# Other first fillers on TensorE, another order of VectorE's work, and a filler moved, in a state-space block followed by an MLP

## The chip, the cores and the metric

The kernel runs on one core of a Trainium2 chip. Its time is the device time of one execution in microseconds; of several executions the median counts. A profiled execution also gives a trace: what each engine did, when, and what it waited for. The engines are TensorE (PE, with its weight loads as PEld), VectorE (DVE), ScalarE (ACT), GpSimd (POOL) and SyncE (SP, which only issues DMAs here). They run side by side, each through its own queue in order, and wait for each other by semaphores.

## The reference

Two blocks one behind the other, all in float32 (`S` = 768, `D` = 32, `N` = 16, 4 batches of 8 heads):

```python
log_a = np.log(np.clip(a, 1e-06, 1.0))
for c in range(nc):                          # chunks of 32 steps
    cum = np.cumsum(la, axis=-1)
    L = np.exp(cum[:, :, :, None] - cum[:, :, None, :]) * causal
    M = np.einsum('bhin,bhjn->bhij', Cc, Bc) * L
    y_intra = np.einsum('bhij,bhjd->bhid', M, xc)
    y_inter = np.einsum('bhin,bhnd->bhid', Cc, state) * np.exp(cum)[..., None]
    y[:, :, sl] = y_intra + y_inter
    state = decayed state + sum over the chunk of B x, decayed to its end
h = x @ w_in                                 # x: y as (3072, 256); w_in (256, 2048)
g = h * (1.0 / (1.0 + np.exp(-1.702 * h)))
return (g @ w_out).astype(np.float32)        # w_out (2048, 256)
```

The weights reach the kernel as 64-bit floating-point numbers, as pairs of 32-bit words.

## The kernel before

The 3072 tokens are worked in 6 groups of 512 (128 steps of all four batches). The kernel uses chunks of 64 steps instead of 32, which gives the same result. For a group, the first block gives `yT`, the transposed input of the second; the second makes 16 blocks of 128 hidden columns from it (`hidden`, L791 for the first group) and projects them to the output. From the second group on, the matrix products are split by a scheme of seven products instead of eight, with sums of operands made by VectorE (`first`, `product`, L847 to L956). The first group has plain products, because the weights are still being prepared.

No scheduler decides the order: the kernel is written in the order in which each engine is to run, and `in_order` ties each engine's instructions to that order. The order below is therefore the order in each queue.

**The start, on TensorE.** `dense` (L424) multiplies a matrix of ones by itself, in float32, into a bank that nothing reads afterwards or, with `start=False`, into unused columns of a bank in use; `pads` (L417) does so with 4 columns and a 32x32 tile. At L1056 to L1067 the queue is: two `dense` of 192 columns, the eight mask products (`mask`, L500, 16-bit operands), three `dense`, 27 `pads`. Then `differ_of(0)` and `differ_of(1)` (L506), which read the running sums `cum` that VectorE scans (L362), `rows_first` (L495), `score` (L604, result `cb`) and `turn_back` (L562). Float32 products show two records each in the trace.

**The exponents.** ScalarE takes `decay_exp` (L536) of the differences, once for the first pair of batches and four times for the second; VectorE multiplies the result with `cb` (`weigh`, L615), which gives `L`.

**The rows.** `finish(range(PG), (0,))` and `(1,)` make the first group's `yT`. Step 0 is a `dense` of 256 columns and `intra` of the first pair (L729; its two halves t = 0, 1 of the heads go to different banks). Step 1 is, for each t, `intra` of the second pair, a copy by ScalarE (`copied`, L741), `inter` (L716, needs the state that `gain`, L635, and `keep_first`, L651, make) and another copy. At t = 0 a second `dense` of 256 columns stands behind `intra`. The banks of t = 1 were those of `turn_back`, which VectorE reads in `ends_first` (L467, result `Be`); so `intra` of t = 1 waits for `Be`.

**The weights.** `fetch` loads the weights in ten pieces; the first six hold `w_in`, of 2, 2, 2, 2, 4 and 4 blocks. Piece 0 comes in two halves of one block each. The 64-bit numbers are taken apart and rounded to float32 with integer and float operations: `fields` step 0 cuts out the exponent field (L203, into `p`), step 1 the top of the mantissa (L206, into `m`), `rounded` adds the low word (L222), `clamp` (L215, L217) moves the exponent to the float32 range on ScalarE, and `join` puts in the sign (L236) and multiplies (L242, into `w_in`). A memset of one element on VectorE ahead of a load (`held`, L170) sets when SP may issue it. The exponents of piece 0 are handled in two halves: field and clamp of half 0 ahead of `ends_first`, field and clamp of half 1 behind it (L1098 to L1103).

Of the kernel before, what the change touches and what calls it, by code (L numbers as in the profile page):

```python
# [8 lines left out]
FP32 = mybir.dt.float32  # L9
# [7 lines left out]
P = 128  # L17
# [18 lines left out]
def kernel(  # L36
# [154 lines left out]
    def columns(i, half):  # L191
        n = PIECES[i][2] * DM
        return slice(0, n) if half is None else slice(half * n // 2, (half + 1) * n // 2)

    def fields(i, steps=range(2), half=None):
        cols = slice(0, PIECES[i][2] * DM)
        if i not in power:
            mantissa[i] = wide.tile([P, PN], U32, tag="m", name=f"m{i}")[:, cols]
            power[i] = wide.tile([P, PN], U32, tag="p2", name=f"p2{i}")[:, cols]
        cols = columns(i, half)  # L200
        hi = bits[i][1][:, cols]
        if 0 in steps:
            nc.vector.tensor_scalar(out=power[i][:, cols], in0=hi, scalar1=0x7FF00000, scalar2=None,  # L203
                                    op0=ALU.bitwise_and)
        if 1 in steps:
            nc.vector.tensor_scalar(out=mantissa[i][:, cols], in0=hi, scalar1=0x000FFFFF,  # L206
                                    scalar2=0x00100000, op0=ALU.bitwise_and, op1=ALU.bitwise_or)

    def clamp(i, steps=range(2), half=None):


        e = power[i][:, columns(i, half)]
        z = e.bitcast(FP32)
        if 0 in steps:
            nc.scalar.activation(z, e, AF.Relu, scale=-8.0, bias=edge[:, 0:1])  # L215
        if 1 in steps:
            nc.scalar.activation(e, z, AF.Relu, scale=-1.0, bias=edge[:, 1:2])  # L217

    def rounded(i, half=None):

        cols = columns(i, half)
        nc.vector.scalar_tensor_tensor(out=mantissa[i][:, cols].bitcast(FP32), in0=bits[i][0][:, cols],  # L222
                                       scalar=2.0 ** -32, in1=mantissa[i][:, cols],
                                       op0=ALU.mult, op1=ALU.add)
# [192 lines left out]
    def pads(n, t, start=True):  # L417

        for i in range(n):
            c = 32 * (i % R)  # L420
            nc.tensor.matmul(out=t[c:c + 32, :4], lhsT=ones[:32, :32], rhs=ones[:32, :4],
                             start=start, stop=True, tile_position=(0, c), skip_group_check=True)

    def dense(t, n=4, start=True):  # L424
        nc.tensor.matmul(out=t[:, :n * H], lhsT=ones,
                         rhs=ones[:, :H].unsqueeze(1).to_broadcast([P, n, H]),
                         start=start, stop=True, skip_group_check=True)

    def decay_heads(p, r, ab):

# [33 lines left out]
    def ends_first(p):  # L464

        t = ssd.tile([P, R, 2 * Q, N], FP32, tag="Be", name=f"Be{p}", bufs=3)
        nc.vector.tensor_tensor(  # L467
            out=t, in0=rb[p], in1=drops[:, p].unsqueeze(3).to_broadcast([P, R, 2 * Q, N]), op=ALU.mult)
        BE[p] = t.rearrange("p r (k q) n -> p k r (q n)", k=2), t
# [140 lines left out]
    def weigh(p, ks=(slice(0, 2),)):  # L610

        Lv = Ls[p].rearrange("p k r q i -> p k r (q i)")
        cb = st[p]["cb"].rearrange("p r k e -> p k r e")
        for k in ks:
            nc.vector.tensor_tensor(out=Lv[:, k], in0=Lv[:, k], in1=cb[:, k], op=ALU.mult)  # L615
# [66 lines left out]
    def finish(pairs, steps=range(2)):  # L682


        g, first = divmod(pairs[0], PG)
        early = pairs[0] < PG
        if 0 in steps:
            if early:
                banks = begun_y["banks"] = [bank(f"y0_{i}") for i in range(4)]
                y = [t[:, :2 * P].rearrange("p (k i) -> p k i", i=H) for t in banks]  # L690
                begun_y[0] = [[y[2 * t + i] for t in range(NK)] for i in range(2)], set()
            else:
                both = area(f"y{pairs[0]}")[:, :, :len(pairs) * 2 * H].rearrange(
                    "p (s t) (k i) -> p s t k i", s=2, i=H)
                begun_y[pairs[0]] = [[both[:, i, t] for t in range(NK)] for i in range(2)] + [both], set()
        y, begun = begun_y[pairs[0]]

        def begin(i, t, parts):
            new = not begun & {(i, t, q) for q in parts}
            begun.update((i, t, q) for q in parts)  # L700
            return new

        def inter(n, p, ts=range(2)):

            b = place(p)[1]
            for k in range(2):
                for i in range(2):
                    if g == 0 and i == 0:
                        continue
                    old = (state[g][:, 0] if i else state[g - 1][:, 1])[:, b + k]  # L710
                    for r in range(R):
                        t = r // 2
                        if t not in ts:
                            continue
                        rows, to = slice(32 * r, 32 * r + 32), Q * D * (r % 2)
                        nc.tensor.matmul(  # L716
                            out=y[i][t][to:to + Q * D, 2 * n + k], lhsT=old[rows],
                            rhs=st[p]["CsT"][rows, k, SIDES[i]],
                            start=begin(i, t, range(Q * (r % 2), Q * (r % 2) + Q)), stop=early,
                            tile_position=(32 * r, to), skip_group_check=True)  # L720

        def intra(n, p, ts=range(2)):
            L = Ls[p]
            for k, t in [(k, t) for t in ts for k in range(2)] if early else [
                    (k, t) for k in range(2) for t in ts]:
                for q in range(HB):
                    h = t * HB + q
                    for i, side in enumerate(SIDES):
                        nc.tensor.matmul(  # L729
                            out=y[i][t][D * q:D * q + D, 2 * n + k], lhsT=rx[p][side, k, h],  # L730
                            rhs=L[side, k, h // Q, h % Q],
                            start=begin(i, t, (q,)), stop=not early, tile_position=(H * i, D * q),
                            skip_group_check=True)

        cols = slice(2 * first * P, 2 * (first + len(pairs)) * P)

        if first == 0 and g not in yT:
            yT[g] = ffn.tile([P, NK, TG], FP32, tag="yT", name=f"yT{g}")
        if early:
            def copied(i, t):  # L740
                nc.scalar.activation(  # L741
                    yT[g][:, t, cols].rearrange("p (k s i) -> p s k i", s=2, i=H)[:, i], y[i][t],
                    AF.Copy)

            if 0 in steps:
                dense(begun_y["banks"][0][:, 2 * P:])
                intra(0, pairs[0])
                return
            for t in range(NK):
                intra(1, pairs[1], (t,))  # L750
                if t == 0:
                    dense(begun_y["banks"][0][:, 2 * P:])
                copied(0, t)
                for n, p in enumerate(pairs):
                    inter(n, p, (t,))
                copied(1, t)
        else:
            for step in steps:
                for n, p in enumerate(pairs):
                    (inter, intra)[step](n, p)  # L760
            if 1 not in steps:
                return
            for i in range(2):
                nc.scalar.activation(  # L764
                    yT[g][:, :, cols].rearrange("p t (k s i) -> p s t k i", s=2, i=H)[:, i], y[2][:, i],
                    AF.Copy)
        state.pop(g - 1, None)
        for p in pairs:
            st.pop(p)
            Ls.pop(p)  # L770
# [283 lines left out]
        differ(p, [(r, ab[p, r]) for r in range(R)])  # L1054

    busy = bank("busy")  # L1056
    for k in range(2):
        dense(busy, 3)
    both = area("ab0")
    for r in range(R):  # L1060
        mask_banks(0, r, both[:, r])
    seconds = [bank(f"ab1_{r}") for r in range(R)]
    for r in range(R):
        mask_banks(1, r, seconds[r])
    for r in range(3):
        dense(both[:, r, 2 * P:], 3, False)
    pads(27, both[:, 0, 2 * P:], False)  # L1067
    differ_of(0)
    turn_blocks(0, "C")
    fetch(0, held=nc.vector, halves=(0,))  # L1070
# [24 lines left out]
    weigh(0, (slice(0, 1),))  # L1095
    fetch(1, held=nc.vector)
    weigh(0, (slice(1, 2),))
    fields(0, (0,), 0)  # L1098
    clamp(0, half=0)
    for p in range(PG):  # L1100
        ends_first(p)
    fields(0, (0,), 1)
    clamp(0, half=1)  # L1103
    for i in range(2, 6):
        fetch(i, held=nc.vector if i == 2 else None)
    rows = a.rearrange("b h s -> (b h) s")
# [10 lines left out]
    keep_first(0)  # L1117
    finish(range(PG), (1,))
    join(0, 2, (0,))
    fields(0, (1,), 1)  # L1120
    rounded(0, 1)
    join(0, 2, (1,))
    fields(1)
    clamp(1)
# [240 lines left out]
```

## Time and profile before

| what | value |
|---|---|
| median of 3 runs | 352.63 us (351.96 to 353.89) |
| the profiled execution | 349.35 us |
| its span, first to last instruction | 347.6 us |
| TensorE busy | 341.9 us, 98% |
| VectorE busy | 256.2 us, 74% |
| ScalarE busy | 150.2 us, 43% |
| GpSimd busy | 46.0 us, 13% |
| granted TensorE clock | 0.999 |
| TensorE's first product, first product of `hidden` | 1.21 us, 17.27 us |

In a line of the timeline the first number is the start in us from the beginning of the span, the second the length, then engine, line, operation, output and inputs, shape and how many records were merged; in brackets, how long the engine had been idle before, and what released it. TensorE's products overlap, so a merged line is somewhat longer than its records are apart. A line of the chain of waits has start, length, and the work or wait that decided there. The page's slices (8.7 us each) show VectorE busy at nine tenths or more from 17.4 to 87 us, and the DMA engines from 17.4 to 52 us.

### The profile page before, as it was taken

To read this page: it belongs to the slowest core of one execution; us is meant where nothing else is said; L and a number is where in the kernel's file an instruction comes from. 1 tells how busy PE (TensorE), PEld (TensorE's weight loads), DVE (VectorE), ACT (ScalarE), POOL (GpSimd) and SP (SyncE) were. 2 spreads that over 40 slices of the span, in tenths; PEclk is the share of its full clock that TensorE was granted. 3 is DMA by queue.
4 is the path that set the end of the run, shared out by engine and by line. 5 is a ranking of instruction groups with operands and counts; after the bars stand their busy time and mean duration, and the time that the engine had idled before them with its cause. 6 is when DMAs were issued, how large, how long until landed. Compare 5 with 4: busy or idle time off the path is not lost.

```text
span 347.6 us, 8544 instructions
## 1 busy us (share of the span) xinstructions
PE 341.9 (98%) x3514; PEld 281.7 (81%) x3514; DVE 256.2 (74%) x479; ACT 150.2 (43%) x335; POOL 46.0 (13%) x82
## 2 busy tenths in 40 slices
PE   8899999999999999999999999999999999999996
PEld 7668964555788888888888888888888888899996
DVE  7799999999699897839985648985554653555463
ACT  6689664005354314644332543442444322554320
POOL 8306810300495000000000000000000000000000
PEclk9999999999999999999999999999999999999999
DMA  4799995713638000474123345120000120000221
GB/s 106 220 297 287 286 158 126 117 25 76 101 87 139 2 0 17 78 136 80 29 35 64 44 102 98 24 32 7 2 4 0 19 35 9 0 2 0 33 31 60
DMA packets 82831, 25.79 MB, mean 74 GB/s; under 512 B 68856, under 2 KB 81144, under 8 KB 82792
## 3 DMA queue, kind: packets, MB, share of 16 engines
q1 hardware_dynamic: 79912, 23.19, 31.5%
q0 software_dynamic: 1888, 1.74, 2.8%
q8 instruction: 27, 0.44, 0.5%
q10 hardware_dynamic: 992, 0.33, 0.4%
q14 instruction: 12, 0.10, 0.1%
HBM read 21.99 MB, written 3.24 MB: 73 GB/s over the span
## 4 chain that ended last, share of the span: by engine, by line
PE 90%; DVE 5%; DMA 2%; issue 1%; SPq 0%; DVEq 0%
PE acc L949 28%; PE X L847 19%; PE Y L857 14%; PE o L889 8%; PE acc L956 7%; PE h L791 6%; PE y L729 2%; PE cb L604 2%; PE y L716 2%; DMA bits<-in_moe_w_in_dram 1%; PE A L635 1%; DVE p L236 1%; DVE p L203 1%; DVE w_in L242 1%; DMA zC<-in_C_dram 1%
## 5 line engine op out<-in xcount | busy, mean ns | idle before, releaser
L852 ACT ACTIVATE ac<-X 128x256 f32<-128x256 f32 x76 | 29.1, 383 | 79.8 <-PE X L847 79.4
L949 PE MATMUL acc<-mg,mw 128*128 128x256 f32 x192 | 54.5, 379 | 0.0
L976 DVE TENSOR_TENSOR gT<-Y,ac 128x512 f32<-128x512 f32 x38 | 26.2, 690 | 37.1 <-PE Y L857 33.3
L824 ACT ACTIVATE gT<-gT 128x512 f32<-128x512 f32 (+1 forms) x76 | 39.3, 519 | 31.6 <-DVE gT L976 31.0
L847 PE MATMUL X<-my,mi 128*128 128x256 f32 x152 | 45.1, 379 | 0.0
L976 DVE TENSOR_TENSOR gT<-Y,b 128x256 f32<-128x256 f32 x38 | 15.8, 418 | 34.4 <-PE Y L857 34.4
L949 PEld LDWEIGHTS acc<-mg,mw 128*128 128x128 f32 x192 | 36.5, 190 | 5.0
L791 PE MATMUL h<-yT,w_in 128*128 128x128 f32 (+2 forms) x186 | 36.3, 353 | 0.2 <-DVE w_in L242 0.2
L949 PE MATMUL acc<-gT,w_out 128*128 128x256 f32 x128 | 35.5, 379 | 0.0
L791 PEld LDWEIGHTS h<-yT,w_in 128*128 128x128 f32 x186 | 27.1, 191 | 8.4 <-issue 5.5
L847 PEld LDWEIGHTS X<-my,mi 128*128 128x128 f32 x152 | 28.0, 190 | 3.7
L889 PE MATMUL o<-gT,w_out 128*128 128x512 f32 x64 | 28.6, 597 | 0.0
L815 DVE TENSOR_TENSOR mg<-gT 128x512 f32<-128x512 f32 x40 | 27.2, 680 | 0.0
L949 PEld LDWEIGHTS acc<-gT,w_out 128*128 128x128 f32 x128 | 24.2, 190 | 3.4 <-ACT yT L764 0.2
L852 ACT ACTIVATE b<-X 128x256 f32<-128x256 f32 x38 | 14.6, 384 | 20.6 <-PE X L847 20.2
L847 PE MATMUL X<-yT,w_in 128*128 128x256 f32 x76 | 23.2, 389 | 0.0
L857 PE MATMUL Y<-yT,w_in 128*128 128x256 f32 x76 | 22.7, 381 | 0.0
L857 PE MATMUL Y<-my,mi 128*128 128x256 f32 x76 | 22.6, 379 | 0.0
L847 PE MATMUL X<-my,w_in 128*128 128x256 f32 x76 | 22.6, 381 | 0.0
L857 PE MATMUL Y<-yT,mi 128*128 128x256 f32 x76 | 22.5, 379 | 0.0
L889 PEld LDWEIGHTS o<-gT,w_out 128*128 128x128 f32 x64 | 11.8, 190 | 13.2 <-issue 12.7
L1008 POOL DMA_DIRECT2D out_dram<-ob x32 | 17.4, 551 | 26.8 <-DVE ob L1003 26.1
(142 smaller groups left out, 580.2 us busy)
## 6 DMA issues: line engine op xcount, KB each, us to landing
a<-scratch SPq DMA_DIRECT2D x18, 256.0 KB
bits<-in_moe_w_out_dram SPq DMA_DIRECT2D x8, 512.0 KB
x<-in_x_dram SPq DMA_DIRECT2D x20, 128.0 KB
bits<-in_moe_w_in_dram SPq DMA_DIRECT2D x8, 256.0 KB
bits<-in_moe_w_in_dram SPq DMA_DIRECT2D x4, 512.0 KB
out_dram<-ob SPq DMA_DIRECT2D x128, 16.0 KB
af<-in_a_dram SPq DMA_DIRECT2D x20, 64.0 KB
zC<-in_C_dram SPq DMA_DIRECT2D x36, 32.0 KB
```

The lines of the kernel that those rows point to most:

```text
L604: nc.tensor.matmul(out=s["cb"][side, r, k].rearrange("p (q i) -> p q i", q=Q), lhsT=BT[rows, k, side], rhs=CT[rows, k, :, side], start=Tru ...
L791: nc.tensor.matmul(out=h[:, cols], lhsT=w_in[:, f, k], rhs=yT[g][:, k, cols], start=(k == 0 and e == 0), stop=(k == NK - 1), skip_group_ch ...
L815: nc.vector.tensor_tensor(out=t[:, 0:2], in0=B[:, :, 1], in1=B[:, 0], op=ALU.subtract)
L824: nc.scalar.activation(o, i, AF.Silu, scale=GELU_SCALE)
L847: nc.tensor.matmul(out=s["X"], lhsT=lhsT, rhs=rhs, start=i == "1", stop=i == "4", skip_group_check=True)
L852: nc.scalar.activation(copy, s["X"], AF.Copy)
L857: nc.tensor.matmul(out=o, lhsT=lhsT, rhs=rhs, start=s.pop("new", False), stop=i != "5", skip_group_check=True)
L889: nc.tensor.matmul(out=o[c], lhsT=w_out[:, c, f], rhs=gT[g, f // 2][:, f % 2], start=(f == 0), stop=(f == NF - 1), skip_group_check=True)
L949: nc.tensor.matmul(out=acc[g][0][i], lhsT=w, rhs=h, start=(j == 0 and (i, 0) in begins), stop=(j == NF // 2 - 1), skip_group_check=True)
L956: nc.tensor.matmul(out=o[k] if type(o) is list else o[:, cols], lhsT=h[:, cols], rhs=w, start=(j == 0 and (i, k) in begins), stop=(j == NF ...
L976: nc.vector.tensor_tensor(out=o, in0=v, in1=w, op=ALU.add)
L1008: (nc.sync if g else nc.gpsimd).dma_start(out=rows[:, b, :, cols], in_=t[32 * r:32 * r + 32, b * P:(b + 1) * P].rearrange("p (u e) -> p u ...
```

## The change

Four edits at the start of the kernel:

1. The first fillers. Both groups of `dense` in front of and behind the masks (2 and 3 float32 products of 192 columns) give way to `plain`: 6 products of 256 columns each, of a 16-bit constant 1.0 that the framework writes (POOL memset, from 0.38 us). One pad fewer (26).
2. `ends_first` of both pairs now stands ahead of the exponent field and clamp of piece 0's half 0.
3. The field of half 1 is cut out together with its mantissa, behind `join` of half 0, and its clamp is made by two VectorE operations (`clamp_here`) behind its rounding, instead of two ScalarE activations.
4. The second 256-column `dense` goes from step 1 of `finish` (behind `intra` of the second pair, t = 0) to step 0: a `dense` now stands before each half t of `intra` of the first pair.

The instructions of the other engines, and the DMAs, keep their order. The parameter `engine` of `fields` is used with its default only.

```diff
--- before.py
+++ after.py
@@ -192,7 +192,7 @@
         n = PIECES[i][2] * DM
         return slice(0, n) if half is None else slice(half * n // 2, (half + 1) * n // 2)
 
-    def fields(i, steps=range(2), half=None):
+    def fields(i, steps=range(2), half=None, engine=nc.vector):
         cols = slice(0, PIECES[i][2] * DM)
         if i not in power:
             mantissa[i] = wide.tile([P, PN], U32, tag="m", name=f"m{i}")[:, cols]
@@ -200,11 +200,20 @@
         cols = columns(i, half)
         hi = bits[i][1][:, cols]
         if 0 in steps:
-            nc.vector.tensor_scalar(out=power[i][:, cols], in0=hi, scalar1=0x7FF00000, scalar2=None,
+            engine.tensor_scalar(out=power[i][:, cols], in0=hi, scalar1=0x7FF00000, scalar2=None,
                                     op0=ALU.bitwise_and)
         if 1 in steps:
             nc.vector.tensor_scalar(out=mantissa[i][:, cols], in0=hi, scalar1=0x000FFFFF,
                                     scalar2=0x00100000, op0=ALU.bitwise_and, op1=ALU.bitwise_or)
+
+    def clamp_here(i, half):
+
+        e = power[i][:, columns(i, half)]
+        z = e.bitcast(FP32)
+        nc.vector.tensor_scalar(out=z, in0=e, scalar1=8.0, scalar2=float(896 << 23),
+                                op0=ALU.mult, op1=ALU.subtract)
+        nc.vector.tensor_scalar(out=e, in0=z, scalar1=0.0, scalar2=float(255 << 23),
+                                op0=ALU.max, op1=ALU.min)
 
     def clamp(i, steps=range(2), half=None):
 
@@ -425,6 +434,13 @@
         nc.tensor.matmul(out=t[:, :n * H], lhsT=ones,
                          rhs=ones[:, :H].unsqueeze(1).to_broadcast([P, n, H]),
                          start=start, stop=True, skip_group_check=True)
+
+    def plain(t, n, start=True):
+
+        for i in range(n):
+            nc.tensor.matmul(out=t[:, :2 * P], lhsT=nc.const_aps.tensor(1.0, [P, P], BF16),
+                             rhs=nc.const_aps.tensor(1.0, [P, 2 * P], BF16),
+                             start=start, stop=True, skip_group_check=True)
 
     def decay_heads(p, r, ab):
 
@@ -743,13 +759,12 @@
                     AF.Copy)
 
             if 0 in steps:
-                dense(begun_y["banks"][0][:, 2 * P:])
-                intra(0, pairs[0])
+                for t in range(NK):
+                    dense(begun_y["banks"][0][:, 2 * P:])
+                    intra(0, pairs[0], (t,))
                 return
             for t in range(NK):
                 intra(1, pairs[1], (t,))
-                if t == 0:
-                    dense(begun_y["banks"][0][:, 2 * P:])
                 copied(0, t)
                 for n, p in enumerate(pairs):
                     inter(n, p, (t,))
@@ -1054,17 +1069,15 @@
         differ(p, [(r, ab[p, r]) for r in range(R)])
 
     busy = bank("busy")
-    for k in range(2):
-        dense(busy, 3)
+    plain(busy, 6)
     both = area("ab0")
     for r in range(R):
         mask_banks(0, r, both[:, r])
     seconds = [bank(f"ab1_{r}") for r in range(R)]
     for r in range(R):
         mask_banks(1, r, seconds[r])
-    for r in range(3):
-        dense(both[:, r, 2 * P:], 3, False)
-    pads(27, both[:, 0, 2 * P:], False)
+    plain(both[:, 0, 2 * P:], 6, False)
+    pads(26, both[:, 0, 2 * P:], False)
     differ_of(0)
     turn_blocks(0, "C")
     fetch(0, held=nc.vector, halves=(0,))
@@ -1095,12 +1108,10 @@
     weigh(0, (slice(0, 1),))
     fetch(1, held=nc.vector)
     weigh(0, (slice(1, 2),))
+    for p in range(PG):
+        ends_first(p)
     fields(0, (0,), 0)
     clamp(0, half=0)
-    for p in range(PG):
-        ends_first(p)
-    fields(0, (0,), 1)
-    clamp(0, half=1)
     for i in range(2, 6):
         fetch(i, held=nc.vector if i == 2 else None)
     rows = a.rearrange("b h s -> (b h) s")
@@ -1117,8 +1128,9 @@
     keep_first(0)
     finish(range(PG), (1,))
     join(0, 2, (0,))
-    fields(0, (1,), 1)
+    fields(0, half=1)
     rounded(0, 1)
+    clamp_here(0, 1)
     join(0, 2, (1,))
     fields(1)
     clamp(1)
```

## The prediction

> **What bounds the kernel now.** I read the page first, then the windows by stage, then the timeline of the first 36 us engine by engine, then the chain of waits over the first 60 us.
>
> ```profile
> PE 341.9 (98%) x3514; PEld 281.7 (81%) x3514; DVE 256.2 (74%) x479; ACT 150.2 (43%) x335; POOL 46.0 (13%) x82
> ```
>
> TensorE is busy for 98% of the span, and the windows show why: from 100 to 200 us and from 200 to 300 us it is busy 100.00 of 100.00 us, with the granted clock at 1.00. Nothing there is touched. A change of the first 18 us counts only by how much earlier or later TensorE enters that full stretch. So the question is what last holds TensorE up before it. The chain of waits answers (start, length, what):
>
> ```profile
> 30.95 1.21 DVE w_in L242
> 32.16 0.14 issue
> 32.30 3.72 PE h L791 x20
> ```
>
> From 32.30 on the chain is TensorE alone; before it, back to 13.2 us, it is VectorE, one instruction behind another. The timeline of TensorE has the same place as its last stall:
>
> ```profile
> 26.66 5.45 PE L791 MATMUL h<-yT,w_in 128*128 128x256 f32 x24
> 32.30 3.72 PE L791 MATMUL h<-yT,w_in 128*128 128x256 f32 x20 [0.19 <-DVE w_in L242]
> ```
>
> The 24 records from 26.66 are 256 columns at 0.213 us each (the rate at which such records follow each other there), so the next product could have started at 26.66 + 24 x 0.213 = 31.78. It started at 32.30, behind the ninth weight block (f = 8). TensorE had 0.52 us to spare, VectorE none. **The end of the kernel moves as VectorE's chain of weight preparation moves, from 10.95 to 32.16.** It begins here:
>
> ```profile
> 1.21 1.65 PE L425 MATMUL busy<-ones 128*128 128x192 f32 x4 [1.21 <-DVE ones L316]
> 2.65 1.92 PE L500 MATMUL ab<-below,identb 128*128 128x256 bf16 x8
> ...
> 4.35 1.59 PE L425 MATMUL ab<-ones 128*128 128x192 f32 x6
> 5.17 0.69 DVE L362 TENSOR_TENSOR_SCAN cum<-carry,cum 128x256 f32<-128x256 f32 x1 [0.35 <-ACT cum L358]
> ...
> 5.88 0.62 PE L421 MATMUL ab<-ones 32*32 32x4 f32 x54
> ...
> 6.43 0.69 PE L506 MATMUL ab<-cum,picks 32*64 32x128 f32 x32
> ...
> 10.95 1.29 DVE L615 TENSOR_TENSOR L<-L,cb 128x512 f32<-128x512 f32 x2 [2.26 <-PE cb L604]
> ```
>
> The running sums `cum` end at 5.86, but the products that read them (L506) start at 6.43, because fillers and pads stand ahead of them in TensorE's queue. From L506 to `cb` TensorE is busy without a gap, and VectorE idles 2.26 us for `cb`.
>
> **The change part by part.**
>
> *First fillers.* Today the first products wait for `ones` (1.21). The new ones read a constant that POOL has set by 0.48; the other engines' first instructions start at 0.80 to 0.87, so I take 0.95 for TensorE (bounds 0.85 and 1.21). In narrow windows the 192-column f32 records follow each other every 0.32 us at 1.69, 2.01 and 2.33, the 256-column 16-bit ones (L500) every 0.213 us; from 5.29 the last three f32 records fit into 0.59 us. So TensorE runs at half its later rate until about 5.3 us, though the clock column says 1.00. The new queue: 6 x 0.213 from 0.95 gives 2.23 (both things L500 waits for are there: `below` at 2.06, `identb` at 1.64); 8 x 0.213 gives 3.93; 6 x 0.213 gives 5.21; 52 pads of the 54 that took 0.55 give 5.74. That is ahead of `cum` at 5.86, so L506 starts at about 5.92: 0.51 us earlier, never more in an execution like this one, and nothing at worst (pads at the low rate for twice 0.55, from 5.21 to 6.3, still leave 0.1; no gain at all if the first product stays at 1.2 as well). Does it reach VectorE? `cb` runs 0.51 earlier, from 8.70; its two inputs end at 7.80 (ScalarE) and 8.68 (VectorE, L572). ScalarE's second exponents waited 0.43 for TensorE (9.29) and follow the first ones, which end at 8.86. So L615 starts at 10.44: **-0.51**, bounds 0 and -0.51.
>
> *VectorE's order.* Its start-to-start slots from 10.95 to 17.54 (first operation of the next piece), in us: products with `cb` 0.64 and 0.57, first power field 0.21, `Be` pair 0.67, a wait of 0.17, second field 0.22, products 0.60 and 0.60, then per half mantissa 0.32, rounding 0.34, sign 0.45, weight 0.35: sum 6.59. The wait is visible here: the second field's half of the weights comes in at 13.19.
>
> ```profile
> 13.21 0.29 DVE L203 TENSOR_SCALAR p<-bits 128x256 uint32<-128x256 uint32 x1
> 13.26 0.40 PE L729 MATMUL y<-L,x 64*32 64x64 f32 x24 [0.55 <-DVE Be L467]
> ...
> 14.63 0.29 DVE L206 TENSOR_SCALAR m<-bits 128x256 uint32<-128x256 uint32 x1
> 14.95 0.43 DVE L222 SCALAR_TENSOR_TENSOR m<-bits,m 128x256 f32<-128x256 uint32 x1
> 15.04 0.70 PE L425 MATMUL y<-ones 128*128 128x256 f32 x2
> ```
>
> After the change nothing waits there (the half is first read near 15.2): -0.17. The first field, moved behind `Be`, reads its half near 12.3 instead of 12.16, where it did not wait. The moved fields keep their slots. The two clamp operations are new to VectorE. They are single-input 128x256 operations, nearest to L203 and L206 (0.29 us each); each result is read by the next instruction, as L206's is by L222, whose slot is 0.32. Bounds: 0.21 (the slot of one that nothing waits for) and 0.45 (a two-input one with a reader). Taken 2 x 0.32 = **+0.64**, bounds 0.42 and 0.90. The sum of the slots is 6.59 - 0.17 + 0.64 = 7.06, so +0.47, bounds +0.25 and +0.73. No cover hides this: behind it stand all later pieces, up to f = 8.
>
> *ScalarE* loses two activations of 0.51 us. Its state copies (L651) started at 14.50, as the second clamp ended at 14.59; now `Be` is ready at about 12.4 and they can start near 13.75.
>
> *TensorE between 12 and 17.* The second 256-column filler stood between the last rows' products (ending 15.04) and L716 (15.67), 0.63 us on its own path; it goes into the 0.55 us in which TensorE waited for `Be`. With that, `Be` earlier by 0.21 and the start by 0.51, the first hidden product (17.27) can start near 16.0. But block f = 1 is written near 17.6, f = 2 near 20.4: TensorE then idles about 1 us ahead of f = 2, and is again at VectorE's mercy at f = 8. On the end this is worth **0**; without that bound it would be worth up to -0.52 more than VectorE's shift.
>
> *Loads.* SP's weight loads from the third piece on are released by a small VectorE memset at 13.45, now near 12.6; no queue order changes, and VectorE waits for no landing after 13.2. Also 0.
>
> Sum: -0.51 + 0.47 = **-0.04 us**, bounds -0.26 and +0.73. The profiled execution took 349.35 us (span 347.6, 1.75 around it) and would take 349.3. The median of the runs shown is 352.63, 3.3 above it (351.96 to 353.89); the difference applied to it gives **352.6**.
>
> **Rivals.**
>
> *The gain carries further* (chance 0.25). The half rate may end later in other executions. If it held through the present queue, the second fillers would take 6 x 0.32 and the pads would end at 4.35 + 1.92 + 0.55 = 6.82 or later (up to 7.4 with slow pads), against about 5.9 after: -0.9 to -1.1 instead of -0.51. For it: the half rate does end inside this stretch. [...] A second source: the 1.21 us of the f = 8 block at 30.95 against 0.69 for its like stands beside a POOL clip (30.45 to 33.55) that follows a load; if that moves off, another -0.5. Together -0.4 to -1.2: 351.8; both at their fullest, -0.04 - 0.6 - 0.5 - 0.5 = -1.6, 351.0.
>
> *The start doesn't move, the clamps cost* (0.15): the change does half of what it says. TensorE's first product starts late or the pads run slowly, VectorE keeps its +0.47 to +0.73: 353.2. Against: TensorE has no other wait there.
>
> *Slower: the rate falls back* (0.10). Place: 13 to 17 us, where the 256-column filler at 15.04 is gone and only small tiles remain. The point from which it decides: if small tiles don't hold the rate, the hidden products start at half of it, 0.853 instead of 0.427 us per 512-column record, for as long as the start needed, 4.1 us; that loses 2.05 us, of which the idle 1 us ahead of f = 2 hides half: +1.0, 353.6. If it takes two such stretches, +3.1: 355.7. Against: from 5.88 to 11.26 there are only small tiles too, and the filler at 11.26 still runs at 0.22 per record; for: the two records at 15.04 are 0.32 apart. [...]
>
> **How the numbers follow.** Forecast 0.50, with its own range 352.4 to 353.4; the rivals 0.25, 0.15 and 0.10. A measurement of this kernel tells about 0.5% (1.76 us) from no change. Faster by that needs the first rival at its fullest or the runs' own spread (they lie 1.9 us apart): 0.13. Slower needs the third at two stretches, or the spread: 0.12. Within: 0.75. The range reaches from the first rival's far end, 350.9, to between the third's two prices, 354.3.
>
> **What would show it.** Right: first product below 1.0; L506 near 5.92; L615 near 10.44; two 0.29 us operations on `p` near 17; first hidden product near 16.0, a TensorE gap before f = 2, and f = 8 again waiting for VectorE near 32.3. Wrong: L506 still above 6.3; records of 512 columns 0.85 apart after 16; f = 8 not waiting for VectorE; or f = 8 moved by over 0.8 us either way.

## The result, and the profile after

In the first timing the changed kernel took 350.11 us (median of 5, 350.06 to 350.32), the kernel before 352.49 us (5 runs, 351.96 to 353.89): ratio 0.9929, 95% interval 0.9907 to 0.9951. Timed again beside 33 executions of the kernel before (median 351.08, 349.33 to 354.43), it took 350.25 (11 runs, 350.07 to 350.86): ratio 0.9965 [0.9936, 0.9994]. The change makes the kernel faster, and the second timing, with far more executions, says by less than the first. The kernel before spreads over 5 us. All five of its first runs lie at 351.96 or more, as only 35 of 102 later ones do. At that share five in five have a chance of about 0.005, so the first timing was either unlucky or of a kind that runs long more often; the clocks of those five aren't on record.

The profiled executions say the opposite. Before: span 347.6, time 349.35. After: span 348.4, time 350.11, or 0.8 us **longer**. So the difference is not where one execution of each shows it. First, though, what that pair does show. The page of the changed kernel, busy time by engine:

```profile
PE 341.2 (98%) x3514; PEld 280.0 (80%) x3514; DVE 256.9 (74%) x481; ACT 148.9 (43%) x333; POOL 45.0 (13%) x82
```

VectorE has two instructions more, ScalarE two fewer, and the number of TensorE's records is the same 3514. The timeline of the changed kernel, along the places of the prediction:

```profile
0.84 1.44 PE L441 MATMUL busy<-const-bfloat16-1.0 128*128 128x256 bf16 x6 [0.84 <-PEq L1361]
...
5.89 0.70 PE L522 MATMUL ab<-cum,picks 32*64 32x128 f32 x32 [0.79 <-DVE cum L371]
...
8.73 0.97 PE L620 MATMUL cb<-CT,Bt 32*64 32x128 f32 x47
10.35 0.54 PE L620 MATMUL cb<-CT,Bt 32*64 32x128 f32 x17 [0.65 <-issue]
11.00 1.30 DVE L631 TENSOR_TENSOR L<-L,cb 128x512 f32<-128x512 f32 x2 [2.35 <-PE cb L620]
12.88 0.41 DVE L203 TENSOR_SCALAR p<-bits 128x256 uint32<-128x256 uint32 x1
...
16.66 3.71 PE L806 MATMUL h<-yT,w_in 128*128 128x512 f32 x8
16.74 0.29 DVE L213 TENSOR_SCALAR p<-p 128x256 f32<-128x256 uint32 x1
17.06 0.29 DVE L215 TENSOR_SCALAR p<-p 128x256 uint32<-128x256 f32 x1
17.39 0.43 DVE L245 SCALAR_TENSOR_TENSOR p<-bits,p 128x256 uint32<-128x256 uint32 x1
18.20 0.42 DVE L203 TENSOR_SCALAR p<-bits 128x512 uint32<-128x512 uint32 x1
...
21.24 1.10 PE L806 MATMUL h<-yT,w_in 128*128 128x512 f32 x2 [0.86 <-DVE w_in L251]
...
31.68 1.19 DVE L251 SCALAR_TENSOR_TENSOR w_in<-m,p 128x512 f32<-128x512 f32 x1
33.02 3.72 PE L806 MATMUL h<-yT,w_in 128*128 128x256 f32 x20 [0.31 <-ACT p L226]
```

TensorE reaches the first products that read `cum` at 5.89 instead of 6.43, and `cb` at 8.73 instead of 9.21. Then the gain is gone: behind the 47th record of `cb` it stands still for 0.65 us, released by nothing the profile shows ("issue"), and VectorE begins at 11.00, as before (10.95). The kernel before had a gap behind the same 47th record, ending at 10.29. Its timeline of the weight loads (PEld) shows it, where that of the products merged it away:

```profile
10.29 0.30 PEld L604 LDWEIGHTS cb<-CT,Bt 32*64 32x64 f32 x17 [0.36 <-issue]
```

The two clamps take slots of 0.32 and 0.33 (16.74, 17.06, 17.39). The next piece starts at 18.20 instead of 17.54, and block f = 8 at 33.02 instead of 32.30. There `w_in` ends at 32.87 and ScalarE's clamp at 32.90, so the label names the later of two that end together.

### The profile page after: what moved, and what is told of

Read it like the earlier page. It is cut to its first block, busy times and chain, and to the rows that moved or that the text cites. A ratio compares the mean times of both kernels' runs of the same rounds, so it can differ in the third digit from the quotient of the medians.

```text
span 348.4 us, 8544 instructions
## 1 busy us (share of the span) xinstructions
PE 341.2 (98%) x3514; PEld 280.0 (80%) x3514; DVE 256.9 (74%) x481; ACT 148.9 (43%) x333; POOL 45.0 (13%) x82
## 4 chain that ended last, share of the span: by engine, by line
PE 91%; DVE 4%; ACT 3%; issue 1%; ACTq 1%; DVEq 0%
PE acc L964 28%; PE X L862 19%; PE Y L872 14%; PE o L904 8%; PE acc L971 7%; PE h L806 6%; PE cb L620 2%; PE y L745 2%; PE y L732 2%; PE A L651 1%; ACT p L226 1%; ACT p L224 1%; PE ab L522 1%; DVE m L231 1%; DVE p L245 1%
```

## The experiments

Every kernel here computes the whole reference. "Before" is the median of the kernel before, timed alongside on the same chip. "Low clock" counts executions whose mean granted clock was under 0.997; "the others" are the rest. The runs e1 to e4, e5 to e8, e9 to e11 and e12 were on four different chips, on which the kernel before was low in 10 of 35, 12 of 33, 3 of 17 and 8 of 17 executions.

| run | median (range), executions | ratio to before | low clock | mean of the others |
|---|---|---|---|---|
| kernel before, all four timings | 351.05 (349.23 to 354.43), 102 | 1 | 33, mean 352.67 | 350.46 |
| after, first timing and e5 | 350.22 (350.06 to 350.86), 16 | 0.9965 [0.9936, 0.9994] (e5) | 0 | 350.31 |
| e1 before again | 352.31 (349.35 to 353.98), 12 | 1.0025 [0.9992, 1.0058] | 7 | 350.80 |
| e2 fillers only | 350.03 (349.30 to 352.09), 12 | 0.9978 [0.9947, 1.0009] | 2 | 349.99 |
| e3 order only | 350.61 (349.55 to 351.67), 12 | 0.9993 [0.9968, 1.0018] | 0 | 350.62 |
| e4 moved filler only | 350.31 (349.34 to 351.92), 12 | 0.9983 [0.9956, 1.0009] | 0 | 350.32 |
| e6 fillers + moved filler | 349.79 (349.21 to 350.99), 11 | 0.9957 [0.9923, 0.9990] | 0 | 349.82 |
| e7 no clamps on VectorE | 349.81 (349.02 to 350.92), 11 | 0.9956 [0.9929, 0.9982] | 3 | 349.77 |
| e8 no second filler | 351.66 (349.20 to 353.44), 11 | 1.0009 [0.9974, 1.0044] | 7 | 349.72 |
| e9 e6 without pads | 354.00 (352.39 to 355.40), 6 | 1.0085 [1.0054, 1.0115] | 5 | 352.39 |
| e10 after without pads | 353.73 (350.49 to 355.45), 12 | 1.0076 [1.0047, 1.0106] | 9 | 351.45 |
| e11 e6 with 39 pads | 355.34 (353.86 to 356.44), 6 | 1.0130 [1.0105, 1.0156] | 5 | 353.86 |
| e12 e9 with pads behind `cb` | 351.77 (350.08 to 354.43), 12 | 1.0027 [0.9996, 1.0058] | 11 | 350.08 |

**The parts alone: e1 to e4.** e1 is the kernel before. e2 has the diff's first fillers (`plain(busy, 6)`, `plain(both[:, 0, 2 * P:], 6, False)`, 26 pads) and nothing else; e3 has VectorE's order and `clamp_here` alone; e4 only moves the second 256-column filler:

```
             if 0 in steps:
-                dense(begun_y["banks"][0][:, 2 * P:])
-                intra(0, pairs[0])
+                for t in range(NK):
+                    dense(begun_y["banks"][0][:, 2 * P:])
+                    intra(0, pairs[0], (t,))
...
-                if t == 0:
-                    dense(begun_y["banks"][0][:, 2 * P:])
```

> The kernel before, unchanged. Theory A (TensorE's slow rate at the start lasts longer in most executions than in the one that was profiled, 349.35 us): the times lie again between 351.9 and 353.9 us, and a profile of an execution near 352.5 us shows 192- or 256-column fillers at the slow spacing (0.32 us, or 0.213 us for 16-bit ones) well beyond 5.3 us, or products of the first hidden blocks at 0.85 us per record. Theory B (the profiled execution and the others differ in the loads, not in TensorE's rate): the slow rate ends near 5.3 us again, and the 3 us are found as waits for a load. Theory C (spread of the measurement): some of its executions come near 349.4 us.

> Only the first fillers changed (16-bit constant, one pad fewer); VectorE's order and the filler between the rows as before. Theory A: this alone gives the steady fast start: about 349.5 to 350.0 us, with a narrow spread, 2.4 to 3 us below before. Rival (the filler moved between the rows holds the rate): no gain, 352.5 us with before's spread. Rival (VectorE's order): no gain either.

> Only VectorE's order and the two clamps on VectorE changed; fillers as before. From the record before: 0.47 us more in VectorE's chain, so 352.9 to 353.2 us by theory A, with before's spread. Rival (VectorE's order brings the gain): 350 to 351 us.

> Only the second 256-column filler moved to between the first rows; the rest as before. Theory A: no change at the end, 352.5 us plus or minus 0.3, with before's spread. Rival (that filler keeps TensorE's rate up and before loses it between 13 and 17 us): 350 us, narrow spread.

Expected and measured: e1 came out as its theory C, with executions near 349.4 us and others at 352 to 354. e2 came near its 349.5 to 350.0 but not with a narrow spread, and e3 and e4 missed theory A: both came out where their rivals stood, at 350 to 351. Four ratios between 0.998 and 1.003 settle little; the clock of each execution settles more. In a third of the executions of the kernel before it is low, and those are 2.2 us longer in the mean (352.67 against 350.46). The profile of e2 caught one of them. (The expectations call the low clock "the fall", and so does what follows.) Its windows of 1 us, TensorE's granted clock in the column behind the five engines, then DMA share and GB/s:

```profile
core 0: us, PE busy (x) PEld busy (x) DVE busy (x) ACT busy (x) POOL busy (x), PEclk, DMA share, GB/s
...
14.00:15.00 1.00, 0.72 (x30) 0.43 (x32) 1.00 (x3) 0.97 (x4) 0.00 (x0) 1.00 0.48 129
15.00:16.00 1.00, 1.00 (x18) 0.58 (x15) 0.93 (x4) 0.22 (x1) 0.00 (x0) 0.50 0.89 260
...
20.00:21.00 1.00, 1.00 (x3) 0.37 (x2) 0.00 (x1) 0.95 (x3) 0.00 (x0) 0.50 0.86 238
21.00:22.00 1.00, 1.00 (x3) 0.48 (x2) 0.97 (x3) 1.00 (x1) 0.00 (x0) 0.59 1.03 330
22.00:23.00 1.00, 1.00 (x3) 0.40 (x3) 0.97 (x4) 0.99 (x3) 0.00 (x0) 1.00 1.07 372
```

From 15.0 to about 21.8 TensorE runs at half its clock (0.59 in the window from 21 is 0.82 us at 0.50, so 6.82 us in all). Its timeline shows the same:

```profile
15.25 1.22 PE L425 MATMUL y<-ones 128*128 128x256 f32 x2
16.40 1.12 PE L723 MATMUL y<-CsT,S 32*64 32x64 f32 x16
...
19.10 10.21 PE L798 MATMUL h<-yT,w_in 128*128 128x512 f32 x30
```

The same two filler records take 0.70 us without the fall. The first hidden product comes at 19.10, where the kernel before, profiled without the fall, has 17.27. e3 and e4 had no such execution in 12 each; at the 33 of 102 of the kernel before that has a chance of about 0.01. So each of these two parts, put alone into the kernel before, very likely takes the fall away; e7 below shows that neither does so in every combination. For e2, 2 of 12 cannot be told from a third.

e3 also shows that the slow rate at the start, which the clock column doesn't show, need not end at 5.3: six filler records from 4.35 last 2.13 us there (1.59 before), and VectorE begins at 11.47. And e1 has one more source of spread: VectorE waited 0.96 us for a load until 26.19, and f = 8 started at 33.33 (32.30 in the kernel before).

**Combinations: e5 to e8.** e5 is the changed kernel. e6 leaves VectorE's order as before. e7 is the changed kernel with the second half's field taken early and clamped by ScalarE. e8 is the kernel before without its second 256-column filler. Against the changed kernel, and (e8) against before:

```
# e7
     for p in range(PG):
         ends_first(p)
     fields(0, (0,), 0)
     clamp(0, half=0)
+    fields(0, (0,), 1)
+    clamp(0, half=1)
...
-    fields(0, half=1)
+    fields(0, (1,), 1)
     rounded(0, 1)
-    clamp_here(0, 1)
# e8
-                if t == 0:
-                    dense(begun_y["banks"][0][:, 2 * P:])
```

> The changed kernel again. Theory A2: the kernel before loses its time in two uneven ways, (i) in a third of its executions the granted clock falls to 0.50 for about 6.6 us from 15 us on, (ii) the slow rate of the first fillers ends at different moments; the change takes both away and pays about 0.5 us for two operations more on VectorE. Then: 350.0 to 350.4 us in every execution, mean clock never below 0.996. Rival (the five executions seen were a lucky draw from the same spread): times from 349.5 to 353 us, some at a mean clock of 0.99.

> First fillers and the moved 256-column filler as in the change; VectorE's order and ScalarE's clamps as before. Theory A2: no fall of the clock (mean 1.0 in all executions), no dear clamps: median 349.4 to 349.9, about 0.5 us below the changed kernel. Rival (VectorE's order is what holds the rate): some executions at mean clock 0.99 and 352 us.

> The changed kernel, but the exponent field of the second half cut early and clamped by ScalarE as before; Be still ahead of both fields. Theory A2 with the term +0.47 for VectorE's chain: 349.6 to 349.9 us, 0.4 to 0.5 below the changed kernel, no fall of the clock. Rival (the clamps on VectorE cost nothing because a load or ScalarE sets the pace of the eighth block): the same as the changed kernel, 350.1.

> The kernel before without the second 256-column filler anywhere. Theory A2 (the clock falls when too little of the stretch from about 11 to 15 us is dense work): the fall to 0.50 comes in at least as many executions as before (a third or more), 352 to 354 us in these; the others come near 349.3 to 351, as TensorE's path to the first hidden product is 0.6 us shorter. Rival (the filler standing at 15 us itself, or its place behind a wait, brings the fall): no execution below a mean clock of 0.996.

In e5 no execution fell, as expected, but 3 of 11 took 350.8 to 350.9, above the expected 350.4. e6 and e7 beat both kernels: without clamps on VectorE the mean of the executions without a fall is 349.8, against 350.31 with them (the difference is 0.49 with a 95% interval of 0.34 either way for e6, 0.54 and 0.36 for e7). In e6 the f = 8 block comes 0.54 earlier than in the changed kernel, in TensorE's timeline:

```profile
32.48 1.75 PE L797 MATMUL h<-yT,w_in 128*128 128x256 f32 x7 [0.58 <-DVE w_in L242]
```

e7 met its time, but not its "no fall of the clock": it fell in 3 of 11, though it has both fillers as in the change. Its profile, of an execution without a fall, has a wait that is 0.16 us in the changed kernel:

```profile
16.71 0.68 PE L732 MATMUL y<-CsT,S 32*64 32x64 f32 x16 [0.87 <-ACT S L667]
```

In ScalarE's queue the second pair of clamps stands again ahead of the copies that make `S`. Only the field and the clamps of half 1 tell e7 from the changed kernel, so VectorE's and ScalarE's order counts beside the fillers (3 of 11 against none of 16 has a chance of about 0.06 if there were no difference).

e8 falls in 7 of 11, against none of 12 in e4, where the same filler is moved and not left out. Its four others have a mean of 349.72. So the second filler pays for its 0.63 us on TensorE's path by what it does against the fall.

How long does a fall last? The mean clocks of all 82 low executions of these runs lie in three groups: 21 at 0.994 or 0.995, 58 at 0.989 or 0.990, 3 at 0.984 or 0.985. Half a clock for the 6.8 us of e2 takes 0.0097 from a mean over 350 us, which is the middle group; so the groups are one, two and three stretches of 3.4 us (an estimate from these numbers). The three of e7 are single ones.

What does the fall follow? For each profile the table gives the stretch of 3.41 us, half of the 6.82, between 8.5 and 19.2 in which TensorE is busy least:

| kernels | least busy time in 3.41 us | low clock |
|---|---|---|
| e12; e9; e8; e7; e1; e2; before; e10 | 1.39; 2.22; 2.27; 2.29; 2.30; 2.34; 2.44; 2.50 | 11 of 12; 5 of 6; 7 of 11; 3 of 11; 7 of 12; 2 of 12; 33 of 102; 9 of 12 |
| after (first and e5); e4; e6; e3 | 2.58 and 2.56; 2.64; 2.64; 2.85 | none of 16, 12, 11, 12 |
| e11 | 2.79 | 5 of 6 |

A line drawn near 2.5 of 3.41 us would part them (2.50 and 2.56 stand on its two sides), with e11 an exception, whose profile is of the one execution of six that did not fall. The weak stretch of the kernel before is where it waits for `Be`, in its window here:

```profile
11.75:15.16 3.41, 2.44 (x130) 1.00 0.59 175
```

And the same one in the changed kernel, with the filler moved into that wait:

```profile
11.75:15.16 3.41, 2.88 (x134) 1.00 0.61 176
```

This is an order of one profile per kernel, not a test of the cause: no run changed this busy time and nothing else. That the stretch is half of e2's fall is a choice of the author's. One long wait is not what came before the fall: in e2 TensorE never waited longer than 0.55 us between 8 and 15, and was busy for 2.34 of the last 3.41 us.

**The gap in `cb`: e9 to e12.** "issue" names no cause. The theory of the next four runs is a border in TensorE's stream of instructions. The gap stands behind the same instruction in both kernels, and the change kept the number of instructions ahead of it. So e9 (from e6) and e10 (from the changed kernel) take 96 of TensorE's instructions away ahead of `cb`, e11 adds 52, and e12 takes 96 away as e9 does and puts them back behind `cb`:

```
# e9, e10
-    plain(both[:, 0, 2 * P:], 6, False)
-    pads(26, both[:, 0, 2 * P:], False)
+    plain(both[:, 0, 2 * P:], 10, False)
# e11
-    pads(26, both[:, 0, 2 * P:], False)
+    pads(39, both[:, 0, 2 * P:], False)
# e12, beside e9's
             if 0 in steps:
+                pads(24, begun_y["banks"][0][:, 2 * P:])
                 for t in range(NK):
```

> As e6 (both fillers as in the change, VectorE's order as before), but the 26 pads, 104 of TensorE's instructions, give way to 4 more 16-bit products (8 instructions): 96 instructions fewer ahead of the products of cb. Theory D (the gap of 0.2 to 0.7 us between the 47th and the 48th record of cb, which ends at 10.0 to 10.4 us however early cb began, is TensorE waiting for its next page of instructions): the gap leaves cb and stands 96 instructions later, among the first rows' products or nowhere; cb ends near 10.1 and VectorE's chain starts near 10.2 instead of 10.6; 349.2 to 349.6 us. Rival (cb waits for an operand there): the gap stays behind the 47th record.

> The changed kernel with the 26 pads replaced by 4 more 16-bit products. Theory D: VectorE's chain starts near 10.4 instead of 11.0, all that follows moves with it up to the ninth weight block: 349.6 to 349.8 us against 350.2. Rival: no gain, 350.2; or, if the pads held the slow rate's end, a wider spread above 350.2.

> As e6 with 39 pads instead of 26: 52 instructions more ahead of cb. Theory D: the gap moves 26 records forward, to behind the 21st record of cb (each record is two instructions), and ends at the same moment, 10.0 to 10.4; VectorE's chain starts up to 0.5 us later than in e6 (26 records come behind it instead of 17: about 0.2). Rival: the gap stays behind the 47th record.

> The e9 kernel (fillers 16-bit, second filler moved, VectorE's order as before, the 26 small pads replaced by 4 more 16-bit products), with 24 pads (96 instructions of TensorE) put behind the scores, ahead of the first rows' filler. From there on each TensorE instruction stands at the same count as in e6 (349.79), while in front of it 96 are missing, as in e9 (353.99). Theory (gaps at fixed counts of instructions): the gap stays out of the scores, cb takes 1.21 in one piece and VectorE weighs near 10.5; the gap falls among the pads or directly behind them; the issue waits of TensorE behind 40 us (2.1 in two in e9) are gone again, and without a fall of the granted clock the time is 349.3 to 349.9. Rival 1 (the loss of e9 comes from the fall of the clock at 17 to 24 alone, which the earlier first rows bring): the issue waits behind 40 us may go, but the clock falls again between 15 and 25 in most executions, and the time stays at 351.5 to 354. Rival 2 (the pads' work itself, or the later slow rate, is what counts, not the count of instructions): issue waits behind 40 us stay, and the time is 353 or more.

TensorE's timeline of e10:

```profile
8.83 1.21 PE L620 MATMUL cb<-CT,Bt 32*64 32x128 f32 x64
...
15.95 0.44 PE L745 MATMUL y<-L,x 64*32 64x64 f32 x27 [0.42 <-issue]
```

`cb` now runs in one piece, VectorE begins at 10.15 (11.00 in the changed kernel), and f = 8 starts at 32.09 instead of 33.02. Yet the time is 3.5 us worse, and e9 missed its 349.2 to 349.6 in the same way, at 354.0. Part of that is the fall (5 of 6 and 9 of 12). The waits of e10 between 40 and 350 us show another part (us in total, times, longest), and its chain the places:

```profile
PE y L745 <- issue: 2.0, 2, 1.2
```

```profile
150.43 1.23 issue
...
204.89 0.74 issue
```

The changed kernel has no such wait. By the theory the gaps are the same thing met elsewhere: with 96 instructions fewer ahead, every later one comes 96 sooner in the count, and the border falls into groups of small products at 150 and 205 us. e9 has the same two (1.36 and 0.77).

e12 is the test. Its timeline of TensorE:

```profile
10.47 0.41 PE L421 MATMUL y<-ones 32*32 32x4 f32 x27
12.90 0.36 PE L421 MATMUL y<-ones 32*32 32x4 f32 x21 [2.02 <-issue]
...
17.58 0.44 PE L736 MATMUL y<-L,x 64*32 64x64 f32 x27 [1.72 <-issue]
```

96 instructions are 48 records. Counted from the old place, the 17 left of `cb`, 4 of `b` and 27 pads are 48: the gap stands exactly there. 126 recorded products later comes the next, which is 252 instructions with their weight loads; in e6 the second gap (14.86) stands 126 products behind the first (10.03) as well. The waits behind 40 us are gone, as expected, and the one execution without a fall took 350.08, against 352.39 for the one of e9. The expected time of 349.3 to 349.9 was missed: both gaps in the first rows grew to 1.7 and 2.0 us, TensorE was thin for that long, and the clock fell in 11 of 12 (rival 1 of that text is right on this). In e11 the expected gap behind the 21st record wasn't seen; the slow rate held until 10 us in its profile, TensorE is busy without a gap from 8.50 to 13.16 there, and by the theory `cb` began too late to meet one. It has its own waits at 205 and 260 us (1.65 and 1.40 in its chain).

In the DMA view an instruction packet of 0.02 MB stands 2.3 to 2.9 us ahead of the end of each gap: 7.5 and 10.29 in the kernel before, 7.9 and 10.35 in the changed one, 7.7 and 10.03, then 12.5 and 14.86 in e6, 13.5 and 15.95 in e10, 10.3 and 12.90, then 14.7 and 17.58 in e12. The ends of two gaps in a row are 4.0 (e10), 4.7 (e12) and 4.8 us (e6) apart. In the kernel before the next packet comes at 11.5, 2.8 us ahead of the next border (by the count of 126 near 14.3), and no wait stands there. So it seems that TensorE stands still when it runs through these 252 instructions in less time than the next packet needs, as it can where records start 0.01 to 0.02 us apart (27 pads within 0.41 us in e12, the 64 of `cb` within 1.21). The borders' places are shown by e12; that the packet is what is waited for is inferred from these times.

## Why the prediction was wrong

The forecast was 352.6, the result 350.11, below the range's 350.9. Two things were wrong: the median to which the difference was applied, which decided, and the difference itself.

**The step that failed** is the last of the sum: "The median of the runs shown is 352.63, 3.3 above it (351.96 to 353.89); the difference applied to it gives **352.6**." It takes the 3.3 us as the same before and after. They are not an offset. Of 102 executions 33 had the fall of the clock, worth 2.2 us; the profiled one (349.35) had none, and the three shown all lie at 351.96 or more, where of the 102 nearly all had a fall (32 of 35; the clocks of the three aren't on record, so that they fell is inferred). The changed kernel had no fall in 16. The difference between the two profiled executions, where neither fell, was +0.76 us (350.11 against 349.35) and not -0.04, just beyond its bound of +0.73. So the gain lies in executions of the kernel before that were unlike the profiled one.

**The rival on the wrong side.** "Slower: the rate falls back" had the event and its place (13 to 17 us; in e2 the fall begins at 15.0) and gave it to the changed kernel. It is the kernel before that falls. That small tiles alone bring it, for 4.1 us a time, was the author's estimate: no run shows that cause, and in e2 the fall lasts 6.8 us. The prediction asked what the rate would do without the filler at 15.04; the 0.55 us of waiting at 13.26 that it goes into it counted as time only, not for the rate. e8 (filler left out, 7 of 11 fell) and e4 (filler moved, none of 12) show that it matters and where it stands; e3 (not moved, none of 12) and e7 (moved, 3 of 11) show that it isn't alone in this.

**First fillers, -0.51.** The mechanism was right up to `cb`: first product at 0.84 (taken 0.95), L522 at 5.89 (5.92), `cb` at 8.73 (8.70). The step "So L615 starts at 10.44: **-0.51**" then missed the gap behind the 47th record, which the trace of before showed as 0.36 in the weight loads; "TensorE is busy without a gap" was the reading that failed, and L615 moved by +0.05. Without that gap (e10) VectorE begins at 10.15. Over many executions the fillers do pay: the mean of those without a fall is 349.99 in e2 against 350.46 before, -0.47 with an interval of 0.34 either way. That the slow rate ends late in some executions, as "The gain carries further" says, would explain it (6.5 us in e3's profile); it wasn't measured execution by execution.

**VectorE's order, +0.47.** Right: in the changed kernel's profile 18.20 - 11.00 is 7.20 us against 6.59 before, +0.61, but in e3 and e10, with the same order, the stretch takes 7.06 (11.47 to 18.53) and 7.07 (10.15 to 17.22), as the sum says. The clamps were right (0.65 for 0.64). In the changed kernel the moved field took 0.41 instead of 0.29 (0.28 in e3, 0.30 in e10), which is most of the other 0.14. At f = 8, all parts together, it is +0.72, and e6 to after gives +0.49 in the means.

**The rest** held: the first hidden product at 16.66 (taken near 16.0, with VectorE beginning 0.56 earlier than it did), 0.86 us of idling ahead of f = 2 (taken about 1), f = 8 still bound by the weights' preparation.

**The sum as the runs give it**, in means: fall -0.71 (351.17 to 350.46), moved filler -0.14 (e4), fillers -0.50 (e4 to e6, on different chips), VectorE's order and clamps +0.49 (e6 to after): -0.86, from 351.17 to 350.31. The terms are differences of the table's means, so that they add up is by construction. The moved filler's and the fillers' term are not clear of noise (0.5 and 0.6 either way). What stands on its own is that 33 of 102 executions fell before and none of 16 after, and the price of the clamps.

What stays open: which part of the change takes the fall away (e3, e4 and e6 have none, e2 and e7 have some), whether the least busy stretch is really what brings the fall (e11 speaks against it, from one profile), what sets the end of the slow rate at the start (5.3 us before, 6.5 in e3, 10 in e11), and why the instruction packets come when they do.

## What to carry to other kernels

Before a profiled execution is set against a median, see whether they belong together: a profile 3 us below every timed run is of another kind of execution, and what makes the kinds may be just what the change touches. A filler may be worth more in a wait of TensorE than on its path: here the kernels that fell were, but for e11, those with less than about 2.5 busy us in some 3.41, which is an order seen and not a tested rule. And count TensorE's instructions when adding or dropping small fillers, since 96 fewer at 5 us made waits at 150 and 205 us (1.23 and 0.74 in e10).

## What the runs showed of the hardware that was not expected

The granted clock fell to 0.50 for 6.8 us in the middle of work (e2), with no wait of TensorE above 0.6 us from 8 us up to the fall (0.55 at the most in e2, 0.56 in e8), in a share of the executions that the kernel's detail sets: from none of 16 (after) to 11 of 12 (e12). The mean clocks suggest falls of 3.4 us and of 10 us as well (an estimate from the three groups and the 6.8 us).

In e6 and e12 two gaps in a row stand 126 recorded products apart, 252 instructions with their weight loads, and in runs of small products TensorE stood at such places for 0.2 us (e6) to 2.0 us (e12), until 2.3 to 2.9 us after an instruction packet of 0.02 MB. Where records start 0.01 to 0.02 us apart the profile shows these waits; in the kernel before, the second such place (near 14.3) shows none.
